# A chain of two expert layers in row-tiled matmuls: which signal each wait between the array's halves takes

## The chip, the cores and the metric

The kernel runs on one core of a Trainium2 chip. The metric is the device time of one execution in microseconds (us), the median of several runs. Engines: TensorE (PE, with its weight loads shown as PEld), VectorE (DVE), ScalarE (ACT), GpSimd (POOL) and SyncE (SP). SP does no arithmetic here: it issues DMAs and passes signals.

## What is computed

A causal convolution with softmaxed taps over 4 x 4096 tokens of 192 channels, and then two feed-forward layers on the 16384 tokens; each has an inner width of 2048:

```python
x = conv(x, softmax(weight))              # 7 taps, one set for each of 8 groups of 24 channels
h = np.maximum(x @ w_in, 0.0)             # layer 1: (16384,192) @ (192,2048)
x = h * h @ w_out                         #          (16384,2048) @ (2048,192)
h = x @ moe2_w_in                         # layer 2
g = np.where(h > 0.0, h, np.exp(np.minimum(h, 0.0)) - 1.0)
out = g @ moe2_w_out
```

All of it is float32. The kernel splits each operand of a product into a high and a low part (`Ah`/`Al`, `gh`/`gl`) and adds three products of parts.

## The kernel before, in words

**Blocks and units.** The tokens are cut into 32 blocks of 512 (`j`). One layer of one block is 8 units (`c`), each of which makes 256 of the 2048 inner channels. The list `units` (lines 531 to 536) gives the order: after a beginning, eight units of layer 2 for block j-2 take turns with eight units of layer 1 for block j; at the end stand sixteen units of layer 2. There are 512 units.

**What one unit does (loop of line 631).** PE computes `h` = x @ w_in of unit u into two PSUM banks (`gemm1`, line 379) and, three units late (`LAG`), adds g @ w_out of unit u-3 into two more banks, `yA` and `yB` (`gemm2`, line 396). Then ACT and DVE make g of unit u: ACT `r` = relu(h) (line 458), for layer 2 ACT `exp` (462), DVE `make_g` (469 for layer 1, 471 for layer 2; 471 also reads h), ACT `gh` (611), DVE `gl` (617). The tile `h` has two buffers, so the products into h of unit u wait until `make_g` of unit u-2 has read its buffer. In between, one or two tasks of a list `bg` run: taps of the convolution, transposes, the folding and splitting of y.

**Two halves of the array.** From unit 32 on (`HALVES`; 480 units) each product of 128 rows is cut into two of 64 rows, one for each half of the array, and the two halves work on different banks at the same time. Each half has 19 products; line 433 issues them in pairs k = 0 to 18, one for half 0 and one for half 1 (`(k, half)` below). By `TURNS`:

- half 0: k 0 to 5 into yA, 6 to 11 into h's bank 0, 12 to 15 into yB, 16 to 18 into h's bank 1;
- half 1: k 0 to 3 into yB, 4 to 9 into h's bank 1, 10 to 15 into yA, 16 to 18 into h's bank 0.

So at three places a half begins on a bank on which the other half was at work: (10, 1) on yA, after (5, 0); (16, 0) on h's bank 1, after (9, 1); and (0, 0) of the next unit on yA, after (15, 1). There the code places waits. After the products of half 1 with k in `SIGNALS` = 5, 11, 15 it puts a `nop` on SP that waits for that product (line 440), and the products in `WAITS` wait for a nop. A product's wait stands on its weight load, which PE takes in the order of the program.

**What else is queued on SP.** Up to three DMA issues (line 645) stand behind a unit's nops and ahead of the next unit's: loads of x (270, 274), moves of x1 (362), stores (513). The nops pass through this same queue in order.

Of the kernel before, what the change touches and what calls it, by code (L numbers as in the profile page):

```python
# [40 lines left out]
def conv_moe_moe_kernel(  # L41
# [17 lines left out]
    nc = tc.nc  # L59
# [360 lines left out]


    TURNS = (("A", 0, "B", 1), ("B", 1, "A", 0))
    SIGNALS, WAITS = (5, 11, 15), ((0, 0), (10, 1), (16, 0))
    SYNC = mybir.DependencyInfo(mybir.DependencyClass.Sync, mybir.DependencyReason.DATA)
    signal = None

    def products(first, second, halves):

        nonlocal signal
        if first and second and halves:  # L430
            work = {**first, **second}
            todo = [[w for what in TURNS[half] for w in work[half, what]] for half in range(2)]
            for k, pair in enumerate(zip(*todo)):
                for half, (w, x, o, st, sp) in enumerate(pair):
                    p = slice(half * DB, (half + 1) * DB)
                    m = nc.tensor.matmul(o, w[p], x[p], start=st, stop=sp)  # L436
                    if signal and (k, half) in WAITS:
                        tc.add_manual_dep(m.ins, signal.ins.name, SYNC, reason="the other half's products")
                    if half and k in SIGNALS:
                        signal = nc.sync.nop()  # L440
                        tc.add_manual_dep(signal.ins, m.ins.name, SYNC, reason="the halves' products")
            return
        for do, parts in ((first, (0, 1)), (second, ("A", "B"))):
            for part in parts if do else ():
                order = (0, 1) if part in (0, "A") else (1, 0)
                begins, ends = (do[half, part] for half in order)
                for (w, x, o, st, _), (_, _, _, _, sp) in zip(begins, ends):
                    nc.tensor.matmul(o, w, x, start=st, stop=sp and part in ("A", "B"))
            if do is first and first:
                for k in range(3, 6):  # L450
                    for half in range(2):
                        w, x, o, _, _ = first[half, half][k]
                        p = slice(half * DB, (half + 1) * DB)
                        nc.tensor.matmul(o, w[p], x[p], start=False, stop=k == 5)  # L454
# [124 lines left out]
    with tc.manual_schedule():  # L579
# [51 lines left out]
        for u in range(NU + LAG):  # L631
# [8 lines left out]
            if 0 <= v:  # L640
                second = gemm2(*units[v], *gsplit.pop(v))
            products(u < NU and first, 0 <= v and second, u >= HALVES)
            for _ in range(3):
                if transfers and transfers[0][0] <= u:
# [70 lines left out]
```

## Time and profile before

| | |
|---|---|
| median of 3 runs | 2571.58 us (2570.11 to 2572.07) |
| the profiled execution | 2571.96 us, span 2570.2 us |
| PE busy | 2437.5 us, 95% of the span |
| PEld (weight loads) busy | 1800.1 us, 70% |
| DVE busy | 1753.9 us, 68% |
| ACT busy | 1504.0 us, 59% |
| mean granted PE clock | 0.990 |

The span runs from the first to the last instruction. A timeline row gives start, length, engine, line and operation, output<-inputs, shape and count, and in brackets the engine's idle time before it and what ended that. Matmuls follow one another in a pipeline, so that their rows overlap: the distance from start to start tells the rate.

### The profile page before, as it was taken

The numbers are of one execution on the slowest core, as the hardware profiler recorded it, in microseconds if no ns is written. First come the engines' busy times: TensorE is split into PE (matmuls) and PEld (weight loads), VectorE is DVE, ScalarE is ACT, GpSimd is POOL, SyncE is SP. The second block draws the span as 40 slices with busy tenths as digits, with TensorE's granted clock in tenths as the row PEclk, the third lists the DMA queues.
The fourth block names the chain that finished last, engine by engine and source line by source line (L and its number), as shares of the span: only waits on it lengthen the run. The fifth ranks groups of instructions, "written<-read, shape, count | busy, mean of one in ns | idle before, by whom it ended". The sixth has DMA issues, their size and how long they took to land.

```text
span 2570.2 us, 44506 instructions
## 1 busy us (share of the span) xinstructions
PE 2437.5 (95%) x18948; PEld 1800.1 (70%) x18948; DVE 1753.9 (68%) x2053; ACT 1504.0 (59%) x1641; POOL 127.0 (5%) x132
## 2 busy tenths in 40 slices
PE   4879999999999999999999999999999999999997
PEld 2556777777777777777777777777777777777775
DVE  7976666666766666766666666666676667676654
ACT  4566566655566655556655556655556655556654
POOL 5544000000000000000000000000000000000000
PEclk8989999999999999999999999999999999999999
DMA  3211100010000010010000010001000001010000
GB/s 90 78 52 28 17 15 13 11 18 16 15 17 12 11 17 16 15 17 11 13 16 17 14 17 11 13 15 18 13 17 11 15 14 18 13 18 5 11 7 13
DMA packets 222615, 49.02 MB, mean 19 GB/s; under 512 B 206544, under 2 KB 220880, under 8 KB 222416
## 3 DMA queue, kind: packets, MB, share of 16 engines
q1 hardware_dynamic: 221312, 46.05, 9.3%
q8 instruction: 148, 2.42, 0.4%
q14 instruction: 51, 0.42, 0.1%
q10 hardware_dynamic: 1104, 0.13, 0.1%
HBM read 25.17 MB, written 12.58 MB: 15 GB/s over the span
## 4 chain that ended last, share of the span: by engine, by line
PE 90%; DVE 5%; issue 2%; ACT 1%; SPq 1%; DMA 1%; POOL 0%; DVEq 0%; ACTq 0%
PE h L436 44%; PE y2A L436 14%; PE y1A L436 13%; PE y2B L436 9%; PE y1B L436 8%; DVE acc L336 1%; DVE a L176 1%; DVE gl L617 1%; SPq L440 1%; ACT r L458 0%; ACT gh L611 0%; DVE a L187 0%; PE h L454 0%; DVE m L203 0%; DVE a L198 0%
## 5 line engine op out<-in xcount | busy, mean ns | idle before, releaser
L611 ACT CAST gh<-r 128x1024 fp32r<-128x1024 f32 x512 | 537.7, 1050 | 577.5 <-DVE r L471 309.5
L617 DVE TENSOR_TENSOR gl<-r,gh 128x1024 fp32r<-128x1024 f32 x507 | 625.7, 1234 | 339.6 <-ACT gh L611 339.6
L458 ACT ACTIVATE r<-h 128x1024 f32<-128x1024 f32 x512 | 524.8, 1025 | 391.0 <-PE h L436 366.1
L436 PE MATMUL y2A<-gh,wo 64*128 64x512 f32 x1968 | 538.7, 393 | 6.5 <-DVE zA L510 6.5
L436 PE MATMUL y1A<-gh,wo 64*128 64x512 f32 x1872 | 511.5, 393 | 0.0
L471 DVE SCALAR_TENSOR_TENSOR r<-r,h 128x1024 f32<-128x1024 f32 x256 | 311.6, 1217 | 285.8 <-ACT r L462 285.2
L436 PEld LDWEIGHTS y2A<-gh,wo 64*128 64x128 f32 x1968 | 364.3, 185 | 52.4 <-issue 7.3
L469 DVE SCALAR_TENSOR_TENSOR r<-h,r 128x1024 f32<-128x1024 f32 x232 | 283.8, 1223 | 165.3 <-ACT r L458 165.3
L436 PEld LDWEIGHTS y1A<-gh,wo 64*128 64x128 f32 x1872 | 346.3, 185 | 43.3
L436 PE MATMUL h<-x2Ah,wiAh 64*128 64x512 f32 x992 | 316.6, 442 | 27.0
L436 PE MATMUL h<-x1Ah,wiAh 64*128 64x512 f32 x928 | 295.9, 441 | 25.2
L436 PE MATMUL y2B<-gh,wo 64*128 64x512 f32 x984 | 308.6, 393 | 0.0
L436 PE MATMUL y2B<-gl,wo 64*128 64x512 f32 x984 | 307.8, 392 | 0.0
L436 PE MATMUL y2A<-gl,wo 64*128 64x512 f32 x984 | 307.8, 392 | 0.0
L436 PE MATMUL h<-x2Ah,wiAl 64*128 64x512 f32 x992 | 294.5, 395 | 0.0
L436 PE MATMUL y1B<-gh,wo 64*128 64x512 f32 x936 | 292.9, 392 | 0.0
L436 PE MATMUL y1B<-gl,wo 64*128 64x512 f32 x936 | 292.5, 392 | 0.0
L436 PE MATMUL y1A<-gl,wo 64*128 64x512 f32 x936 | 292.4, 392 | 0.0
L436 PE MATMUL h<-x2Al,wiAh 64*128 64x512 f32 x992 | 292.4, 393 | 0.0
L462 ACT ACTIVATE r<-r 128x1024 f32<-128x1024 f32 x256 | 271.6, 1061 | 7.8
L436 PE MATMUL h<-x1Ah,wiAl 64*128 64x512 f32 x928 | 275.5, 394 | 0.0
L436 PE MATMUL h<-x1Al,wiAh 64*128 64x512 f32 x928 | 273.4, 392 | 0.0
(126 smaller groups left out, 4839.9 us busy)
## 6 DMA issues: line engine op xcount, KB each, us to landing
xinA<-in_x_dram SPq DMA_DIRECT2D x128, 64.0 KB, 2.3
out_dram<-zA SPq DMA_DIRECT2D x128, 64.0 KB, 1.9
raw<-in_moe_w_out_dram SPq DMA_DIRECT2D x16, 384.0 KB, 3.2
x1Bh<-x1Bh SPq DMA_DIRECT2D x64, 64.0 KB, 1.9
x1Bl<-x1Bl SPq DMA_DIRECT2D x64, 64.0 KB, 1.9
out_dram<-zB SPq DMA_DIRECT2D x64, 64.0 KB, 2.0
xinB<-in_x_dram SPq DMA_DIRECT2D x124, 32.0 KB, 2.1
raw<-in_moe_w_in_dram SPq DMA_DIRECT2D x8, 384.0 KB, 3.3
```

Source lines behind the costliest of these rows:

```text
L176: nc.vector.tensor_scalar(out=self.a.bitcast(U32), in0=hw, scalar1=3, scalar2=0x3FFFFFFF, op0=ALU.logical_shift_left, op1=ALU.bitwise_and,)
L336: nc.vector.scalar_tensor_tensor(out=st[i], in0=t[:, k : k + n], scalar=cw[:, k : k + 1], in1=st[i], op0=ALU.mult, op1=ALU.add)
L436: m = nc.tensor.matmul(o, w[p], x[p], start=st, stop=sp)
L440: signal = nc.sync.nop()
L458: nc.scalar.activation(out=r, in_=h, func=AF.Relu, scale=1.0 if layer == 1 else -1.0)
L462: nc.scalar.activation(out=r, in_=r, func=AF.Exp, scale=-1.0)
L469: nc.vector.scalar_tensor_tensor(out=r, in0=h, scalar=0.0, in1=r, op0=ALU.max, op1=ALU.mult)
L471: nc.vector.scalar_tensor_tensor(out=r, in0=r, scalar=-1.0, in1=h, op0=ALU.add, op1=ALU.max)
L611: nc.scalar.copy(out=gh, in_=gs[u])
L617: eng.tensor_tensor(out=gl, in0=gs.pop(u), in1=f32(gsplit[u][0]), op=ALU.subtract)
```

## The change

`WAITS` becomes a map from the waiting product to the k of the signal that it takes, and `signals` keeps each of a unit's three nops by its k until its one taker has it. Before, `signal` was one name for the nop given last.

```diff
-    SIGNALS, WAITS = (5, 11, 15), ((0, 0), (10, 1), (16, 0))
+    SIGNALS, WAITS = (5, 11, 15), {(10, 1): 5, (16, 0): 11, (0, 0): 15}
     SYNC = mybir.DependencyInfo(mybir.DependencyClass.Sync, mybir.DependencyReason.DATA)
-    signal = None
+    signals = {}
 
     def products(first, second, halves):
 
-        nonlocal signal
...
                     m = nc.tensor.matmul(o, w[p], x[p], start=st, stop=sp)
-                    if signal and (k, half) in WAITS:
-                        tc.add_manual_dep(m.ins, signal.ins.name, SYNC, reason="the other half's products")
+                    after = signals.pop(WAITS.get((k, half)), None)
+                    if after:
+                        tc.add_manual_dep(m.ins, after.ins.name, SYNC, reason="the other half's products")
                     if half and k in SIGNALS:
-                        signal = nc.sync.nop()
-                        tc.add_manual_dep(signal.ins, m.ins.name, SYNC, reason="the halves' products")
+                        signals[k] = nc.sync.nop()
+                        tc.add_manual_dep(signals[k].ins, m.ins.name, SYNC, reason="the halves' products")
```

In the order of the program, (10, 1) took the nop of k = 5 before and takes it now. (16, 0) took the nop of k = 15, given just ahead of it, and now takes that of k = 11. (0, 0) of the next unit is asked to wait for the nop of k = 15 in both; before, (16, 0) of the unit ahead had already waited for that same nop.

## Rows read from the trace of the kernel before

**Rows 1.** The page: busy time of the engines, and the chain that ended last.

```profile
PE 2437.5 (95%) x18948; PEld 1800.1 (70%) x18948; DVE 1753.9 (68%) x2053; ACT 1504.0 (59%) x1641; POOL 127.0 (5%) x132
...
PE 90%; DVE 5%; issue 2%; ACT 1%; SPq 1%; DMA 1%; POOL 0%; DVEq 0%; ACTq 0%
```

**Rows 2.** Busy time by stage: window, length, busy us (instructions), granted clock, DMA share, GB/s.

```profile
1040.00:1440.00 400.00, 390.98 (x3166) 291.18 (x3164) 273.12 (x313) 236.61 (x250) 0.22 (x2) 1.00 0.09 15
```

**Rows 3.** Waits of the weight loads: total us, times, longest us.

```profile
PEld h L436 <- SPq L440: 260.8, 480, 0.6
```

**Rows 4.** Timeline of PE, one unit from k = 0 to the next.

```profile
1500.15 0.39 PE L436 MATMUL y2A<-gh,wo 64*128 64x512 f32 x1
...
1501.32 0.40 PE L436 MATMUL h<-x2Ah,wiAl 64*128 64x512 f32 x1
...
1502.49 0.39 PE L436 MATMUL y2A<-gh,wo 64*128 64x512 f32 x1
...
1502.72 0.40 PE L436 MATMUL y2A<-gh,wo 64*128 64x512 f32 x1
...
1503.65 0.39 PE L436 MATMUL y2A<-gl,wo 64*128 64x512 f32 x1
1504.15 0.19 PEld L436 LDWEIGHTS h<-x2Ah,wiAh 64*128 64x128 f32 x2 [0.54 <-SPq L440]
1504.16 0.49 PE L436 MATMUL h<-x2Ah,wiAh 64*128 64x512 f32 x2
...
1504.49 0.40 PE L436 MATMUL h<-x2Ah,wiAl 64*128 64x512 f32 x2
...
1504.72 0.40 PE L436 MATMUL h<-x2Al,wiAh 64*128 64x512 f32 x2
...
1504.96 0.39 PE L436 MATMUL y2A<-gh,wo 64*128 64x512 f32 x1
```

**Rows 5.** The instructions of line 440 on SP: duration ns min/median/max, first and last start.

```profile
L440 SPq EVENT_SEMAPHORE  x960: 17/22/28, 242.0 to 2556.1; - x192
```

**Rows 6.** Line 436 between 254.2 and 255.2: a wait instruction of PE's queue, and products.

```profile
L436 PEldq EVENT_SEMAPHORE  x1: 51/51/51, 254.4 to 254.4; - x1
...
254.43 0.50 PE L436 MATMUL h<-x2Ah,wiAh 64*128 64x512 f32 x2
...
254.77 0.39 PE L436 MATMUL h<-x2Ah,wiAl 64*128 64x512 f32 x2
```

**Rows 7.** Timeline of ACT in eight units of layer 2.

```profile
1485.94 1.03 ACT L458 ACTIVATE r<-h 128x1024 f32<-128x1024 f32 x1 [0.35 <-PE h L436]
...
1490.41 1.17 ACT L479 COPY yt<-y1B 64x512 f32<-64x512 f32 x2
1491.61 1.03 ACT L458 ACTIVATE r<-h 128x1024 f32<-128x1024 f32 x1
...
1496.49 1.02 ACT L458 ACTIVATE r<-h 128x1024 f32<-128x1024 f32 x1
...
1500.85 1.02 ACT L458 ACTIVATE r<-h 128x1024 f32<-128x1024 f32 x1
```

**Rows 8.** Timeline: the last product into an h, and the ACT instruction that reads it.

```profile
1509.53 0.40 PE L436 MATMUL h<-x2Al,wiAh 64*128 64x512 f32 x2
...
1509.97 1.03 ACT L458 ACTIVATE r<-h 128x1024 f32<-128x1024 f32 x1 [0.22 <-PE h L436]
```

**Rows 9.** Timeline of DVE: make_g and gl of the unit whose r started at 1496.49.

```profile
1498.64 1.22 DVE L471 SCALAR_TENSOR_TENSOR r<-r,h 128x1024 f32<-128x1024 f32 x1 [0.70 <-ACT r L462]
1500.98 1.23 DVE L617 TENSOR_TENSOR gl<-r,gh 128x1024 fp32r<-128x1024 f32 x1 [1.12 <-ACT gh L611]
```

**Rows 10.** Timeline: three DMA issues on SP; their unit's (16, 0) starts at 1484.93.

```profile
1484.93 0.49 PE L436 MATMUL h<-x2Ah,wiAh 64*128 64x512 f32 x2
1485.01 1.11 SPq L362 DMA_DIRECT2D x1Bh<-x1Bh  x2
...
1486.25 0.50 SPq L362 DMA_DIRECT2D x1Bl<-x1Bl  x1
```

## Prediction, made before the change was built

> **What bounds the kernel now.** I read the page first: PE is busy for 95% of the span and makes 90% of the chain that ended last [rows 1]. So PE sets the time, and the question is whether its busy time is dense. The table of stages says 390.98 busy of 400 us in a steady stretch, at the full granted clock [rows 2]: by busy time, only 2.3% is idle. That is where a reader can be misled, since matmul rows overlap. Of the waits of the weight loads one line stands out: 480 waits, one in each unit with halves, 260.8 us in all, for SP's line 440, the nops that the change touches [rows 3].
>
> So I look at one unit, from start to start [rows 4]. From k = 0 (1500.15) to k = 15 (1503.65) lie 15 steps in 3.50 us: 0.2335 us for a pair. Then the row of the weight load of (16, 0) says that it stood 0.54 us for SP's line 440; it begins at 1504.15, 0.50 us after the start of (15, 1), whose end it had to learn of by way of SP. The products of k = 16 start at 1504.16, of k = 17 at 1504.49, and from there the step is 0.23 again (1504.72, 1504.96). From k = 15 to k = 17 it takes 0.84 us instead of two steps, 0.47. So each unit loses **0.37 us**: 0.27 to the wait and 0.10 to filling the pipeline again. The unit lasts 4.81 us; 19 undisturbed steps would be 4.44.
>
> The Trainium skill (Perfetto Trace Analysis, "Per-instruction lifecycle", Tensor Engine) says that a matmul's end in the trace is computed and not observed, and that its semaphore fires after that. The rows agree: the load starts 0.11 us after the end that the row of (15, 1) gives. I use no ends of matmuls in the sum.
>
> **The change, part by part.**
>
> *(10, 1)* takes the same signal as before: nothing. It also shows what a signal costs that is asked for five pairs late: (5, 1) starts at 1501.32, (10, 1) at 1502.49, which is 1.17 us or five steps with no stall [rows 4].
>
> *(16, 0)* now asks for the signal of (11, 1). That product starts at 1502.72; undisturbed, (16, 0) would start five steps later. Its weight load is taken one step ahead of its product, so four steps, 0.93 us, are there for a path that took 0.50 from start to load. This is the same lead as that of (10, 1), so the stall should go: 480 x 0.37 = **177.6 us** off. From the rounding of the rows (0.36 to 0.38) it is 173 to 182.
>
> *(0, 0)* had in effect no wait of its own for the halves, since (16, 0) had already waited for the nop of k = 15. Now it has. From (15, 1) to the weight load of (0, 0) there are three steps, 0.70 us, and the path takes 0.50. So 0.20 us is left; I put it at nothing. Behind this load stands the whole unit on PE, and after it ACT's `r`, so the cover matters: if it is gone, whatever the signal is late by is paid in every unit, with up to 0.10 for refilling.
>
> *The added wait instruction.* (0, 0) also waits for ACT's gh. If its load can't hold both waits, a wait instruction of its own comes ahead of it. The trace of before has such a one on this line: 51 ns at 254.4, between the products of k = 16 and 17, which there start 0.34 us apart (254.43, 254.77) [rows 6] against 0.33 in the unit above [rows 4]. So its price is between 0 and 0.01 us, 0 to 5 us in all; I take 0, because the unit with it also starts k = 16 from a standstill, as the other does. The Trainium skill (Perfetto Trace Analysis, "Identifying Dependency Chains") says the same of instructions that wait for several engines: semaphore instructions may be put ahead of them.
>
> *SP.* Line 440 shows 960 instructions, two for each unit, though the code gives three signals [rows 5]: the nop of k = 11, for which nothing waited, has no row of its own. Now it has a taker, so there should be 1440, each some 0.02 us: nothing. The nop of k = 5 stands behind up to three DMA issues. In the unit of [rows 10] these end at 1486.75, 2.33 us after the start of (15, 1) (0.51 ahead of 1484.93). With no stall, (5, 1) of the next unit starts nine steps, 2.10 us, after (15, 1), and the load of (10, 1) is due after thirteen, 3.03. SP is free 0.70 us ahead of that, and from a free SP to the load it takes less than the 0.50 of the whole path. So this too is nothing.
>
> *What is late next.* ACT's loop in layer 2 is r, exp, (make_g on DVE), gh, r. Without tasks it takes 4.36 us (1496.49 to 1500.85) [rows 7], less than the new unit of 4.44. But two units of the eight carry the folding of y1: their loops take 5.67 (1485.94 to 1491.61, with 1.17 of copies) and 4.88 (to 1496.49) [rows 7]. At 4.44 per unit ACT falls behind by 1.23 and then by 0.44 more, 1.67 in all, and gets back only 0.08 in each later unit of layer 2. That matters through h's two buffers. An h is read from 0.44 us after its last product starts (1509.53 to 1509.97) [rows 8]; make_g ends 3.37 us after r's start (1496.49 to 1499.86) [rows 7, 9]. With the lag its buffer is free 0.44 + 1.67 + 3.37 = 5.48 us after its last pair, plus less than 0.1 for the signal. The next use is (4, 1) two units on, whose load comes 1 + 19 + 3 = 23 steps after that pair, 5.37 us. So PE stands for 0.1 to 0.2 us there, plus up to 0.10 to refill, once per sixteen units; after that the delay has made the room that the rest needs. There are 29 such turns (j = 3 to 31, line 534): 29 x 0.2 = **6 us** back, between 0 and 9. Also gl: it is ready 0.44 + 1.67 + 5.72 = 7.83 us after the pair (1496.49 to 1502.21) [rows 7, 9] and needed 40 steps, 9.34 us, after it: nothing. Layer 1 has no exp in its loop and takes the lag back.
>
> Sum: 2571.96 (the profiled execution) - 177.6 + 6 = 2400.4. The median of the runs is 0.4 below the profiled execution: **2400 us**, 6.7% less.
>
> **The rivals.**
>
> *The lag is paid in full.* If the slack of h's buffers were smaller than I worked out, ACT would set the pace in layer 2. Eight loops there make about 6 x 4.36 + 5.67 + 4.88 = 36.7 us against 35.5 of PE: 1.2 x 29 = 35 us, so 2394 + 35 = 2429. Against it: in the trace of before the lag after the fold caused no stall on PE at all; the only waits of the halves' loads that add up are SP's [rows 3].
>
> *The wait moves to (0, 0).* If the load of (0, 0) can't be taken ahead of its product any more because of its two waits, each unit pays the refill of 0.10: 48 us back, 2448. The loads that wait today after four steps show no such cost (1502.49 starts on time) [rows 4], but none of them waits after only three.
>
> *Only the idle time is to be had.* If the busy share were right, 2.3% of the 480 x 4.81 us is all that could be won: 53 us, 2519. Against it: 15 steps of 0.2335 in a row in every unit.
>
> *It does not do what it says.* If the nop of k = 11 is still put together with that of k = 15 on SP, as 960 instead of 1440 instructions suggest [rows 5], (16, 0) waits as before: 2571. Against it: the nop of k = 5, which has a taker, stands alone today.
>
> *Slower.* SP's queue: the new unit gives SP 0.37 us less between the nop of k = 15 and that of k = 5. If the DMA issues held the nop of k = 5 back, (10, 1) would stop. To make the kernel slower than before, it would have to lose more than 0.37 us in each unit, so SP would have to come free over 3.4 us after (15, 1) in each of them, or later still where only some units have issues; the three issues of [rows 10] are done after 2.33. If they took 3.5 each time, the time would be about 2571.96 + 480 x 0.1 = 2620.
>
> **How the numbers follow.** The forecast of 2400 has 0.84, with a range of its own of 2389 (182 off, no lag paid, less 0.4 for the median) to 2413 (173 off, 5 for wait instructions, 9 for the lag). The lag in full has 0.05, the wait at (0, 0) 0.05, the idle time alone 0.01, no effect 0.03, slower 0.02. The range for 8 in 10 is the forecast's, with some room towards the first rival: 2389 to 2420. About 0.2% is what a measurement of this kernel can tell from no change; faster by more than that comes to 0.95, within it 0.03, slower 0.02.
>
> **What would show it.** Right: the steps from k = 15 to k = 17 are 0.23 like all others, the waits for line 440 are gone from the weight loads' list, line 440 has 1440 instructions, a unit lasts 4.44, and one stop of some 0.2 us for DVE's line 471 shows late in each run of layer 2. Wrong: a stall ahead of k = 0 (the wait has moved), stops at (4, 1) in several units in a row (the lag in full), or at (10, 1) behind DMA issues (SP).

## The result, and the profile after

The changed kernel takes 2400.36 us (median of 4 runs, 2398.28 to 2402.01) against 2571.8 before (four runs): 171.4 us less, a ratio of 0.9334 with a 95% interval of 0.9318 to 0.935. The forecast was 2400 with 2389 to 2420. The profiled execution took 2400.75 us, with a span of 2399.0. In the changed file the products are at line 435 (436 before).

First the page of the kernel after, the two lines that answer to [rows 1], and the stage that answers to [rows 2]:

```profile
PE 2315.8 (97%) x18948; PEld 1935.1 (81%) x18948; DVE 1746.5 (73%) x2053; ACT 1489.1 (62%) x1641; POOL 126.9 (5%) x132
...
PE 82%; DVE 8%; ACT 5%; issue 2%; SPq 1%; DMA 1%; POOL 0%; DVEq 0%; ACTq 0%
```

```profile
1040.00:1440.00 400.00, 399.50 (x3418) 339.49 (x3416) 294.34 (x338) 252.48 (x270) 0.22 (x2) 1.00 0.09 16
```

PE's busy share hardly moves (390.98 to 399.50 us of 400, at a granted clock of 1.00 in both), but in the same 400 us it makes 3418 products instead of 3166. At 38 products per unit that is 4.447 us for a unit instead of 4.801, the stops included: 480 x 0.354 = 170 us, nearly all of the 171. The gain was inside the time that the rows of PE call busy. The smaller share of PE in the chain that ended last (82% after 90%) is no loss of its own: in the run next16 below it is 88%, with a time 2 us longer.

The waits of the weight loads, of the kernel after (total us, times, longest), in place of [rows 3]:

```profile
PEld h L435 <- DVE r L471: 5.5, 25, 0.2
PEld y1A L435 <- SPq L440: 4.0, 7, 0.7
PEld y2A L435 <- SPq L440: 3.7, 8, 0.8
```

The 480 waits, 260.8 us, of (16, 0) are gone. Two small groups are new: 25 loads into h that wait for make_g (line 471), and 15 loads into yA, (10, 1), that wait for line 440 on SP. Line 440 itself, in place of [rows 5]:

```profile
L440 SPq EVENT_SEMAPHORE  x1439: 17/17/17, 241.7 to 2384.5; - x180
```

So all three nops of a unit now stand alone on SP. And the place of the change, in the timeline of PE and its weight loads after; half 0's products and half 1's have rows of their own here:

```profile
1502.35 0.40 PE L435 MATMUL y1A<-gh,wo 64*128 64x512 f32 x1
...
1503.03 0.40 PE L435 MATMUL y1B<-gl,wo 64*128 64x512 f32 x1
1503.03 0.18 PEld L435 LDWEIGHTS h<-x1Ah,wiAh 64*128 64x128 f32 x1
...
1503.27 0.39 PE L435 MATMUL h<-x1Ah,wiAh 64*128 64x512 f32 x1
...
1503.28 0.40 PE L435 MATMUL y1A<-gl,wo 64*128 64x512 f32 x1
...
1503.50 0.40 PE L435 MATMUL h<-x1Ah,wiAl 64*128 64x512 f32 x1
...
1503.73 0.39 PE L435 MATMUL h<-x1Al,wiAh 64*128 64x512 f32 x1
...
1503.83 0.33 PEld L435 LDWEIGHTS y1A<-gh,wo 64*128 64x128 f32 x2
1503.97 0.39 PE L435 MATMUL y1A<-gh,wo 64*128 64x512 f32 x1
```

These are (11, 1); half 0's k = 15; the load of (16, 0) and its product; (15, 1); half 0's 17 and 18; the load of (0, 0) of the next unit and its product. Half 0 steps by 0.23 through (16, 0) and through (0, 0). The reader can see one thing that was not in the trace before: the halves no longer start their pairs together. (16, 0) starts with (15, 1), so half 0 is a step ahead. The stall of before had brought the halves level in each unit. So the leads of (16, 0) and (0, 0) are each a step shorter than the prediction counted: from (11, 1) to (16, 0) lie 0.92 us, four steps and not five, and from (15, 1) to (0, 0) 0.69, three and not four. The load of (16, 0) starts 0.24 us, a step, ahead of its product (1503.03, 1503.27), that of (0, 0) only 0.14 ahead (1503.83, 1503.97): it comes some 0.09 late, and its product is on time all the same. How late a load may be is what the first runs below measure.

The wait instruction that the prediction allowed for is there too, between (15, 1) and (0, 0):

```profile
L435 PEldq EVENT_SEMAPHORE  x1: 51/51/51, 1503.8 to 1503.8; - x1
```

The trace so agrees with what the Trainium skill (Perfetto Trace Analysis, "Identifying Dependency Chains") says of instructions that wait for several engines: semaphore instructions may be inserted ahead of them.

### The profile page after: what moved, and what is told of

The parts are those of the page before. It is cut to its first block, busy times and chain, and to the rows that moved or that the text cites. A ratio compares the mean times of both kernels' runs of the same rounds, so it can differ in the third digit from the quotient of the medians.

```text
span 2399.0 us, 45460 instructions
## 1 busy us (share of the span) xinstructions
PE 2315.8 (97%) x18948; PEld 1935.1 (81%) x18948; DVE 1746.5 (73%) x2053; ACT 1489.1 (62%) x1641; POOL 126.9 (5%) x132
## 4 chain that ended last, share of the span: by engine, by line
PE 82%; DVE 8%; ACT 5%; issue 2%; SPq 1%; DMA 1%; POOL 0%; DVEq 0%; ACTq 0%
PE h L435 38%; PE y2A L435 13%; PE y1A L435 13%; PE y1B L435 8%; PE y2B L435 8%; ACT gh L611 2%; DVE r L471 2%; ACT r L458 1%; DVE gl L617 1%; DVE acc L336 1%; ACT r L462 1%; DVE a L176 1%; SPq L513 1%; DVE r L469 1%; DVE a L187 0%
## 5 line engine op out<-in xcount | busy, mean ns | idle before, releaser
L435 PEld LDWEIGHTS y2A<-gh,wo 64*128 64x128 f32 x1968 | 356.5, 185 | 39.1 <-issue 8.4
L435 PEld LDWEIGHTS y1A<-gh,wo 64*128 64x128 f32 x1872 | 338.0, 184 | 26.0 <-SPq L440 4.0
L435 PE MATMUL h<-x2Ah,wiAh 64*128 64x512 f32 x992 | 311.6, 394 | 0.0
L435 PE MATMUL h<-x2Ah,wiAl 64*128 64x512 f32 x992 | 310.4, 392 | 0.0
L435 PE MATMUL h<-x2Al,wiAh 64*128 64x512 f32 x992 | 310.4, 393 | 0.0
L435 PE MATMUL h<-x1Ah,wiAl 64*128 64x512 f32 x928 | 290.1, 392 | 0.0
L435 PE MATMUL h<-x1Al,wiAh 64*128 64x512 f32 x928 | 290.0, 392 | 0.0
L435 PE MATMUL h<-x1Ah,wiAh 64*128 64x512 f32 x928 | 290.0, 392 | 0.0
```

## The experiments

The theory: each signal takes some 0.47 to 0.50 us from the start of its product to what waits on PE, and a load costs only what it is late by beyond a small allowance; the give-back of some 6 us comes from ACT's lag, as predicted, or from SP's queue, as the new waits above suggest. Two runs test the first part at (16, 0), two at (0, 0), and six the give-back. All changes are against the kernel after.

**How late a signal may be, at (16, 0).** The signal is given for a later product:

```diff
-    SIGNALS, WAITS = (5, 11, 15), {(10, 1): 5, (16, 0): 11, (0, 0): 15}
+    SIGNALS, WAITS = (5, 13, 15), {(10, 1): 5, (16, 0): 13, (0, 0): 15}    # lead13; lead14 has 14
```

> (16, 0) takes the signal of (13, 1) in place of (11, 1): two steps (0.467 us) instead of four are left from that product to the weight load of (16, 0). The load of (0, 0) in the trace after started its wait instruction 0.47 us after (15, 1), so the signal comes 0 to 0.03 us late. Theory (a load can be late by 0.50 - 0.37 = 0.13 us before its product is): 2400 us, within 3. Rival (a load that is late at all loses the refill of 0.10 us): 2400 + 48 = 2448.

Measured: 2398.87 us (2397.24 to 2401.05), as the theory has it. The list of waits has no load of (16, 0) waiting for line 440, and the rival's 48 us are not there.

> (16, 0) takes the signal of (14, 1): one step (0.2335 us) is left. The load comes 0.24 to 0.27 us late. Theory: 0.13 of that is free, so 0.10 to 0.14 us per unit, 2450 to 2466 us. Rival (all lateness counts, and the refill with it): 0.34 to 0.37 per unit, 2563 to 2577.

Measured: 2455.89 us (2455.4 to 2458.08), within the theory's 2450 to 2466 and far from the rival. The waits and the timeline of lead14:

```profile
PEld h L435 <- SPq L440: 144.0, 480, 0.3
```

```profile
1385.19 0.39 PE L435 MATMUL y2A<-gl,wo 64*128 64x512 f32 x1
1385.44 0.19 PEld L435 LDWEIGHTS h<-x1Ah,wiAh 64*128 64x128 f32 x2 [0.30 <-SPq L440]
1385.44 0.50 PE L435 MATMUL h<-x1Ah,wiAh 64*128 64x512 f32 x2
...
1385.78 0.39 PE L435 MATMUL h<-x1Ah,wiAl 64*128 64x512 f32 x2
```

The old picture is back at a smaller size: the load starts 0.25 us after (15, 1) instead of with it, and from k = 15 to 17 it takes 0.59 us instead of 0.47. Of 0.25 us of lateness 0.12 are lost, 480 x 0.12 = 58 us; before the change, 0.37 of 0.50 were lost [rows 4]. So in both some 0.13 us are free: that much of the step by which a load goes ahead of its product can be missed without loss.

**The same at (0, 0), where a wait instruction stands ahead of the load:**

```diff
-    SIGNALS, WAITS = (5, 11, 15), {(10, 1): 5, (16, 0): 11, (0, 0): 15}
+    SIGNALS, WAITS = (5, 11, 16), {(10, 1): 5, (16, 0): 11, (0, 0): 16}    # next16; next17 has 17
```

> The signal that (0, 0) of the next unit takes is given for (16, 1) in place of (15, 1): two steps are left to its weight load, which has a wait instruction of its own ahead of it (51 ns, 0.076 to the load's start). The load comes 0.47 + 0.076 - 0.467 = 0.08 us late, less than the 0.13 that are free. Theory: 2400 us, within 3. Rival (two waits on a load take away that it goes ahead of its product): 0.10 or more per unit, 2448 and above.

Measured: 2402.44 us (2402.27 to 2402.63), as the theory has it, at its upper edge; it is 2 us more than the kernel after, whose slowest run took 2402.01, and where these come from is not shown.

> As next16, for (17, 1): one step is left. The load comes 0.47 + 0.076 - 0.234 = 0.31 us late, 0.18 of it paid: 2400 + 88 = 2488 us by the theory. That is about 30 us more than lead14, whose load has no wait instruction ahead of it; if that instruction costs nothing even here, the two come out alike (2450 to 2466).

Measured: 2502.06 us (2499.87 to 2502.51), 14 us more than the theory, and 46 more than lead14 instead of 30. The timeline of next17:

```profile
1410.80 0.42 PE L435 MATMUL h<-x1Ah,wiAl 64*128 64x512 f32 x2
1411.04 0.42 PE L435 MATMUL h<-x1Al,wiAh 64*128 64x512 f32 x2
1411.41 0.47 PE L435 MATMUL y1A<-gh,wo 64*128 64x512 f32 x1
...
1411.72 0.39 PE L435 MATMUL y1A<-gh,wo 64*128 64x512 f32 x1
```

From k = 18 to the next unit's 0 and 1 it takes 0.37 + 0.31 = 0.68 instead of 0.47: 0.21 lost, 480 x 0.21 = 101 us. The wait instruction costs nothing while its signal is in time, and next to lead14 a unit loses about 0.08 to 0.09 us more where it is not (46 us, less some 5 of stops on SP, told below, that lead14 hardly has, over 480 units). That all of this is the instruction's price is not shown, as the two runs wait at different places. In the kernel after, the load of (0, 0) uses 0.09 of the 0.13 that are free, because half 0 runs a step ahead there. In next16, where the signal is given one product later, half 0 is only 0.04 us ahead (median of the units; 0.23 in the kernel after), and the median unit lasts 4.433 us in both.

**Where the 6 us went: SP's queue taken out.**

```diff
-                        signals[k] = nc.sync.nop()
+                        signals[k] = nc.gpsimd.nop()
```

> The three nops go to POOL's queue, which is idle here, in place of SP's, where they stand behind DMA issues. In the trace after, 14 units stand at (10, 1), 5.5 us in all, behind an issue on SP that took 1.0 to 2.1 us. Theory (SP's queue is where most of the give-back of 6 us went): those stops go, the long issues stay and harm nobody, 2400.4 - 5.5 = 2395. Rival (the lag of ACT takes the give-back, as the prediction had it): 2400.

Measured: 2396.15 us (2395.28 to 2396.82), 4.2 below the kernel after. The waits of pool, and the length of its issues of line 274 (ns, min/median/max):

```profile
PEld h L435 <- DVE r L471: 6.7, 30, 0.2
```

```profile
L274 SPq DMA_DIRECT2D xinB<-in_x_dram x124: 311/448/1552, 9.7 to 2125.9; - x124
```

There is no wait for line 440 any more, while long issues still happen on SP and hold nothing. The waits for make_g are all still there. So the SP part of the give-back is about 4 to 5 us.

**Fewer issues in a row, and more.**

```diff
-            for _ in range(3):
+            for _ in range(2):    # two; six has range(6)
                 if transfers and transfers[0][0] <= u:
                     transfer()
```

> At most two DMA issues per unit on SP in place of three. With one issue of the usual 0.5 and one long one of 2.1 us SP is free 0.43 + 0.07 + 0.5 + 2.1 = 3.1 us after (15, 1), about when the load of (10, 1) is due (3.03). Theory (SP's queue): most of the 5.5 us at (10, 1) goes, 2395 to 2397. Rival (the lag): 2400.

Measured: 2395.77 us (2395.59 to 2396.29), as the theory has it. But it does so in another way than I had expected: I had reckoned with one long issue of 2.1 us behind an ordinary one, and the longest issue of the steady stretch now takes 0.61 us.

> Up to six DMA issues per unit on SP. Theory: six issues of 0.5 us end 0.43 + 3.0 = 3.4 us after (15, 1), the load of (10, 1) is due at 3.03, so each full chain costs some 0.3 us, and a long issue in any of the chains costs 1 to 2. There are two full chains and two of four per sixteen units: 29 x 2 x 0.3 = 17 us, and some 20 long issues at 1.5 us, less the 5.5 paid already: 2430 to 2445. Rival (SP's queue has room): 2400.

Measured: 2426.73 us (2424.82 to 2427.61): slower by 26, near the theory's low end but 3 us below it. The loads of (10, 1) in six:

```profile
PEld y2A L435 <- SPq L440: 33.5, 39, 2.1
PEld y1A L435 <- SPq L440: 7.0, 8, 1.4
```

47 loads wait, 40.5 us in all, against 15 and 7.7 in the kernel after. This is the mechanism of the prediction's "slower" rival, run at twice the dose: it is real, and it is far from the 171 us at stake.

**Both remedies:** the nops on POOL and two issues per unit.

> Both remedies at once: nops on POOL's queue and two DMA issues per unit. Theory (both take away the same stops): 2395 to 2396, no better than either. Rival (two separate losses): 2391 or below.

Measured: 2396.25 us (2394.85 to 2396.79). No better than either, so both take away the same stops.

**ACT's lag.** The exp is left out:

```diff
-                if layer == 2:
-                    act_exp(rs[u])
```

> The exp of layer 2 is left out (g is then made from relu(-h) itself), so ACT's loop in layer 2 is 1.06 us shorter and never falls behind PE for long. If the lag of ACT takes the 6 us of the prediction: 2394. If it takes what the trace after shows, 25 stops with about 1.2 us in all, and 1.3 us more in the last wait near the end: about 1.2 + 1.3 + 1.06 for each of the last two ends of the chain, so 2395 to 2397. If ACT's pace bound layer 2 in full it would be some 30 us less, 2370.

Measured: 2394.61 us (2391.98 to 2397.15). That it is not 2370 shows that ACT's pace does not bound layer 2. Between 2394 and 2395 to 2397 the run can't choose; its interval holds both. Its trace does: no load waits for line 471, yet 16 loads still wait for SP, 8.0 us in all, and the last long wait of yA near the end shrinks (5.4 us instead of 7.6, of which the exp's own 1.06 is a part):

```profile
PE y2A L435 <- issue: 5.4, 1, 5.4
```

With SP's stops in place and the lag gone, the lag's share is what the rows give below, not 6.

**Why some issues on SP are long.** In the kernel before, two issues of the steady stretch took over 1.0 us; in the kernel after, 21 of 508. Two views of after: the timeline around one of them, and the DMA queues while it lasted (packets, MB, share of 16 engines):

```profile
512.28 1.93 SPq L513 DMA_DIRECT2D out_dram<-zA  x1
...
514.33 0.18 PEld L435 LDWEIGHTS y1A<-gh,wo 64*128 64x128 f32 x1 [0.52 <-SPq L440]
```

```profile
q8 instruction: 1, 0.02, 4.4%
```

A 16 KB packet of an instruction queue was under way in each of the 21, and each issue ends 0.24 to 0.42 us after that packet. All 21 are also the third issue in a row on SP; no first and no second one is long. So in this kernel no issue was long without both, the packet and the third place, and both were not always enough: such a packet was under way in 19 issues of ordinary length too, 12 of them the third in a row. The last experiment moves the issues within the unit:

```diff
                     if half and k in SIGNALS:
                         signals[k] = nc.sync.nop()
...
+                    if half and k == 5:
+                        for _ in range(3):
+                            if transfers and transfers[0][0] <= now:
+                                transfer()
...
-            for _ in range(3):
-                if transfers and transfers[0][0] <= u:
-                    transfer()
+            if not (HALVES <= u < NU):
+                for _ in range(3):
+                    if transfers and transfers[0][0] <= u:
+                        transfer()
```

> The up to three DMA issues of a unit stand on SP right behind the nop of k = 5, in place of behind that of k = 15. They start 0.43 us after (5, 1) and last 1.0 to 1.6 us; the nop of k = 11 is due 1.40 + 0.43 us after (5, 1), and the load of (16, 0) 0.5 us later still, so ordinary chains cost nothing. All 21 long issues (1.0 to 2.1 us) of the trace after have a 16 KB packet of an instruction queue in flight, and those packets start about k = 3 to 7 of a unit. Theory (the long issues come from meeting these packets): with the issues at k = 8 to 13 there are few long ones, the stops are nearly gone, 2395 to 2397. Rival (a third issue in a row is slow in itself): some 20 long issues again, which now hold (16, 0), 2400 or more.

Measured: 2399.67 us (2398.49 to 2399.87), which is not the 2395 to 2397 of the theory. Waits of mid:

```profile
PEld h L435 <- SPq L440: 4.3, 8, 0.8
```

Five long issues are left of 21, each again with an instruction packet under way. The number is what the theory wanted, but not for its reason: the issues did not get out of the packets' way, for 50 of them met one, against 40 in the kernel after. 43 of the 50 were the first issue of their unit's up to three, and none of these is long. The rival fails too: no third issue is long here, and the five are second ones. Further, eight loads of (16, 0) now wait, 4.3 us, and three of these eight stand behind ordinary issues: there the issues themselves started late, held by their own waits, so the place is tighter than I had worked out. The time so doesn't decide. What the rows show is that no long issue of these three kernels (before, after, mid) is without an instruction packet, none is the first of its unit, and with at most two issues per unit (two) none is long at all. That the packet holds the issue, and why it does so only behind other issues, is not shown.

## Why the prediction was right, step by step

**The bound and the 0.37 us** held: the wait seen from start to start was the loss, and it went. The rate after is that of an undisturbed step. ACT's r follows PE in layer 1 (timeline of ACT after):

```profile
1513.34 1.03 ACT L458 ACTIVATE r<-h 128x1024 f32<-128x1024 f32 x1 [1.06 <-PE h L435]
...
1517.77 1.03 ACT L458 ACTIVATE r<-h 128x1024 f32<-128x1024 f32 x1 [1.07 <-PE h L435]
```

4.43 us for a unit, where 4.44 was forecast and 4.81 was before.

**(16, 0) and (0, 0)** held: no stall at either. lead13 and next16 show that the signal of either may come later still, by two products and by one; lead14 and next17 show what it costs when the lead is gone. But the leads were counted for halves that stay level. The 0.20 us that the prediction left at (0, 0) is not there in the kernel after: the load comes 0.09 late, and no time is lost because 0.13 of lateness is free, which the prediction had not worked out. *The 177.6 us* is some 2 us small: from nop to nop on SP a unit lasts 4.807 us before and 4.433 after (medians of all 480), 0.374 apart, 179.5 in all.

**"It does not do what it says"** fell with the 1439 instructions of line 440. **"The lag is paid in full"** and **"The wait moves to (0, 0)"** fell with the time, 29 and 48 us below theirs. **"Only the idle time is to be had"** fell with the time: 171 us won where the busy time offered 53.

**SP, "So this too is nothing"**, is the step that failed. I took the issues of one unit, 0.5 us each [rows 10], for what all units do. 21 of 508 took 1.0 to 2.1 us after the change, each the third in a row while a packet of instructions was under way, and 15 loads of (10, 1) waited 7.7 us for it. A load's ordinary distance from the one before (about 0.05, as 0.23 - 0.18) and the 0.13 that are free leave 15 x (0.51 - 0.18) = 5 us; pool and two won 4.2 and 4.6.

**The lag, 6 us**, is a term that was mis-sized. The mechanism is there; the load of (4, 1) waits for line 471 in the unit that was named (timeline of after):

```profile
1549.43 0.18 PEld L435 LDWEIGHTS h<-x2Ah,wiAh 64*128 64x128 f32 x1 [0.23 <-DVE r L471]
```

It happens 25 times in 29 turns, 0.22 us each with the ordinary 0.05. Less the free 0.13 that is 25 x 0.04 = 1 us, not 6: I had charged all of the lateness and a refill on top. One place more I had not listed. Near the end PE waits for yA to be emptied into zA (line 510, DVE); the lag comes on top there. The waits of PE, before and after, and the timeline of after, where the wait is put down to "issue" but the product starts behind zA as it did before:

```profile
PE y2A L436 <- DVE zA L510: 6.5, 1, 6.5
```

```profile
PE y2A L435 <- issue: 7.6, 1, 7.6
```

```profile
2359.94 0.71 DVE L510 STREAM_TRANSPOSE zA<-y2A 128x512 f32<-128x512 f32 x1
...
2360.75 0.76 PE L435 MATMUL y2A<-gh,wo 64*128 64x512 f32 x1 [7.64 <-issue]
```

So the give-back was 5 for SP, 1 for the lag and 1 for the end: 7 us where 6 were forecast, or 8 by the nops (179.5 - 171.4). The sum of 2400 is right partly by luck: two errors in it, of 5 us each, have opposite signs.

## What to carry to other kernels

Where matmul rows overlap, measure from start to start across the place in question, and compare with the undisturbed step; the busy share had 2% to offer where 7% were won. A wait should take the earliest signal that it needs, and a signal of in-order work is worth as much as its lead over the path that it takes: here 0.47 to 0.50 us of path, of which a weight load forgives 0.13. A queue that passes signals should carry nothing that can be slow: two issues per unit instead of three, or the nops on an idle engine's queue, gave another 4 us (2395.8 and 2396.2), the best of the kernels here that compute the whole result.

## What the runs showed of the hardware that I had not expected

- A DMA issue on SP usually takes 0.3 to 0.5 us. Some took 1.0 to 2.1 us, and in the kernels before and after all of these were the third in a row with an instruction packet of 16 KB under way. A change that only moved the work of PE against that of SP brought the long issues from 2 to 21 of 508; the issues that met such a packet went from 12 to 40.
- Freed of the stall, the two halves of the array drift by about a step against each other, with no loss of rate: the median unit lasts 4.433 us with 0.23 between the halves (kernel after) and with 0.04 (next16).
- The busy share of the weight loads says less than it seems: 81% in the kernel after and 91% in lead13 (page of lead13, 2179.6 us), at the same time within 2 us, since the loads of the two halves run at the same time in one and overlap only in part in the other (half 1 is 0.11 us off half 0 there, and a load takes 0.18). The Trainium skill (Perfetto Trace Analysis, "Identifying the Most-Contended Engine") takes that share, beside the share of peak FLOPs and in place of the matmuls' share, as a measure of how near PE is to its limit; with the array in halves it moved by 10 points with no change of the time, and here the rate from start to start decides.
